# Moving the HBM copies of w_in's quarters, and setting the last three of w_out's inner sums behind g's sums

## The chip, the cores and the metric

The kernel runs on one core of a Trainium2 chip. Its engines work side by side, each through its own instructions in order: TensorE (PE in the profile) multiplies matrices, VectorE (DVE) and GpSimd (POOL) do elementwise work, ScalarE (ACT) does activations and copies, SyncE (SP) only issues transfers. Transfers (DMAs) are issued from the queues of SP, GpSimd or ScalarE. An instruction that waits for another engine or for a transfer holds up whatever stands behind it on its own engine. The metric is the device time of one execution in microseconds (us), as a median over runs.

## The reference

A retention layer over 4 batches, 8 heads, 768 steps and a head size of 64, whose output, laid out as 3072 tokens by 512, is the input of a feed-forward block with a quick GELU:

```python
for t in range(S):
    state = gamma[None, :, None, None] * state + np.einsum('bhd,bhe->bhde', k[:, :, t], v[:, :, t])
    y[:, :, t] = scale * np.einsum('bhd,bhde->bhe', q[:, :, t], state)
x = y.transpose(0, 2, 1, 3).reshape(B * S, H * D)
h = x @ w_in                                  # 3072 x 512 by 512 x 2048
g = h * (1.0 / (1.0 + np.exp(-1.702 * h)))
out = g @ w_out                               # 2048 x 512
```

Everything is computed in float32.

## The kernel before

**Blocks.** The tokens are worked through in six blocks (m = 0 to 5) of four chunks each. A chunk is 64 time steps of two batches; `step(j, f)` (L368) lets TensorE attend to chunk j and finish chunk f, with VectorE's mask, state and output operations (L316, L366, L328, L345) and GpSimd's `kd` (L272) and state ageing (L357) beside it; `turn(j)` (L238) has VectorE transpose q and k (L251). Each block needs an up product (x with w_in, giving h), a GELU on ScalarE (L391, giving g) and a down product (g with w_out).

**Fast products.** The products use a seven-product scheme (Strassen in Winograd's form). So sums of quarters of the operands have to be made: of w_in by `sums_w1` (GpSimd, L429), of x by `sums_x` (GpSimd, L439), of w_out by `sums_w2` (VectorE, L445), of g by `sums_g` (VectorE, three operations for each pair of row blocks, L454 to L458) and `sums_g_late` (GpSimd, one for each pair, L460). Blocks 0 and 1 come up in another way during the opening, and go down by `down(m)` (L672); blocks 2 to 5 come up by `up(d)` (L465), d = 0 to 3, a quarter of the product each, and go down by `down49` (L553), which uses the scheme twice over, 49 products, and needs an inner set of sums of w_out.

**`down(m)`.** It is a list of 28 units: seven products (n = 0 to 6) by four quarters d, each unit four matmuls `pd<-W,G` on TensorE (L709; each matmul leaves two records in the profile). The seven are (g0,w0), (g1,w2), (g3,w1), (g0,w5), (g3,w4), (g2,w6) and (g1,w3). After the units of the third (units 8 to 11) `sums_g` is emitted for the pair of that quarter, as it changes g3, g2 and g0 in place; the fourth product (units 12 to 15) reads that g0. After the units of the fifth (units 16 to 19) `sums_g_late` is emitted, which changes g1 for the last product (units 24 to 27). When a product is complete, ScalarE copies it (`keep`, L681) or VectorE adds it to an output tile (`put`, L685, or L716 for `t`), and GpSimd's queue sends the tile out (L686). Output tiles `o` have two buffers. The tile `t`, which the last output sum of a block reads, lies in buffer s1; so does p1, ScalarE's copy of the first product of `up(0)` (L479).

**Inner sums and their transfers.** `inner_w2(i)` (L516), i = 0 to 6, makes three VectorE sums (L522) of one of w_out's seven quarters in X[:, 4:7], and a transfer of 768 KB writes them to HBM, to W2D[i]. All seven share X[:, 4:7], so the sums of i + 1 wait for the transfer of i. The list `INNER` names the block and unit behind which each stands. `inner_w2_t3(i)` (L526) makes a fourth sum in place (L529). In blocks 2 to 5 GpSimd's queue brings W2D back in turn into a tile called ring (L545), which lies where W1B[0] lay; a tile `own`, for sums of g, lies where W1B[1] lay.

**w_in's second half.** W1B[0] and W1B[1] hold the last two of w_in's four parts with their sums. In block 1 `sums_w1` makes these, and SP copies each to HBM (L437, 1792 KB, to W1D). Blocks 3 to 5 fetch them from there (L883, L887).

**Order.** TensorE's instructions run in the order in which they are written. On the other engines a scheduler places them by when it takes them to be ready, except that those passed to `keep_in_program_order` keep theirs. Between units, block 1 also has five pieces of the retention layer (behind units 0 or 2, 5, 11, 16 and 21), and `sums_x` behind the last.

Of the kernel before, what the change touches and what calls it, by code (L numbers as in the profile page):

```python
# [28 lines left out]
def kernel(  # L29
# [29 lines left out]
    pe, act, dve, pool, sp = nc.tensor, nc.scalar, nc.vector, nc.gpsimd, nc.sync  # L59
# [13 lines left out]
    NP = NFF // 2  # L73
# [17 lines left out]
    W1B = [late.tile([P, 2, 7, 2, P], F32, name=f"W1B{i}", tag=f"late{i}") for i in range(2)]  # L91
    W1D = [dram.tile([P, 2, 7, 2, P], F32, name=f"W1D{i}") for i in range(2)]
# [19 lines left out]
    def w1(p):  # L112

        return (W1A, p) if p < NP // 2 else (W1B[p // 2 - 2], p % 2)
# [278 lines left out]
    def g(m, p, s):  # L393

        if m:
            return G[:, p:p + 2, s, :]
        if s < 3:
            t, q1 = w1(p)
            return t[:, q1:q1 + 2, 4 + s].rearrange("p a c f -> p a (c f)")
        return X[:, 4 + p // 2] if p < 6 else G0  # L400
# [28 lines left out]
    def sums_w1(p):  # L429
        t, q1 = w1(p)  # L430
        w = [t[:, q1:q1 + 2, s] for s in range(7)]
        pool.tensor_add(w[4], w[2], w[3])
        pool.tensor_sub(w[6], w[0], w[2])
        pool.tensor_sub(w[5], w[4], w[0])
        pool.tensor_sub(w[2], w[1], w[5])
        if p >= NP // 2:
            sp.dma_start(W1D[p // 2 - 2], W1B[p // 2 - 2])  # L437

    def sums_x():  # L439
        pool.tensor_sub(X[:, 4], X[:, 2], X[:, 0])  # L440
# [19 lines left out]
    def sums_g_late(m, p):  # L460
        a = [g(m, p, s) for s in range(2)]
        tc.keep_in_program_order(pool.tensor_sub(a[1], a[1], a[0]))
# [49 lines left out]
    def w2q(w):  # L512

        return [W2[:, w, u::2, e * P:(e + 1) * P] for u in range(2) for e in range(2)]

    def inner_w2(i):  # L516

        b11, b12, b21, b22 = w2q(ORDER[i][1])
        t = []
        for k, a in enumerate((b12, b22, b21)):  # L520
            t.append(X[:, 4 + k].rearrange("p c (d e) -> p (c d) e", e=P))
            tc.keep_in_program_order(dve.tensor_sub(t[k], a, t[k - 1] if k else b11))  # L522
        tc.keep_in_program_order(sp.dma_start(
            W2D[i].rearrange("p k d e -> p (k d e)"), X[:, 4:7].rearrange("p k c t -> p (k c t)")))

    def inner_w2_t3(i):  # L526
# [21 lines left out]
    def begin_ring():  # L548

        ring = late.tile([P, 7, 4, P], F32, name="ring", tag="late0")  # L550
        return ring, {i: stream(ring, i) for i in range(2)}
# [120 lines left out]
    def down(m):  # L672

        acc, kept = {}, {}
        b, t0 = m * CB // NC * 2, m * CB % NC * D
        rows = out.rearrange("(b t) (e c) -> e t b c", b=B, c=EH)[:, t0:t0 + TH, b:b + 2, :] \
            .rearrange("e (h p) b c -> h e p b c", p=P)

        def keep(name, tag, src):
            kept[name] = one.tile([P, 2, EH], F32, name=name, tag=tag)  # L680
            act.activation(kept[name], src, AF.Copy)  # L681

        def put(th, e, a, b):
            o = two.tile([P, 2, EH], F32, name="o")
            dve.tensor_add(o, a, b)  # L685
            tc.keep_in_program_order((pool if m < NB - 1 else act).dma_start(rows[th, e], o))  # L686

        def last_part(d, halves={}):

            n = d // (NP // 4)  # L690
            if d % (NP // 4) == 0:
                halves[n] = ps.tile([P, EH], F32, name="pd", tag="xy"[n])
            for p in range(NP // 2 * (d % 2), NP // 2 * (d % 2 + 1)):
                pe.matmul(halves[n], g1(m, p, 1)[:, n * P:(n + 1) * P], W2[:, 3, p, :], start=(p == 0), stop=(p == NP - 1))
            if d % 2:
                o = two.tile([P, 2, EH], F32, name="o")
                dve.tensor_add(o[:, 0], halves[n], kept["t"][:, n])
                act.dma_start(rows[0, 1][:, n], o[:, 0])

        def part(key, sa, sb, new, last, d, then):  # L700
            if m == NB - 1 and key == "x2":
                last_part(d)
                return
            if d == 0 and new:
                acc[key] = ps.tile([P, 2, EH], F32, name="pd", tag=key[0])
            p0 = acc[key]
            for p in range(2 * d, 2 * d + 2):
                for n in range(2):
                    pe.matmul(p0[:, n, :], g1(m, p, sa)[:, n * P:(n + 1) * P], W2[:, sb, p, :],  # L709
                              start=(new and p == 0 and n == 0), stop=(last and p == NP - 1), skip_group_check=True)  # L710
            if d == NP // 2 - 1:
                then(p0)

        def then_p5(y):
            kept["t"] = one.tile([P, 2, EH], F32, name="t", tag="s1")
            dve.tensor_add(kept["t"], y, kept["u"])  # L716

        def then_p7(x):
            keep("vv", "s3", x)
            put(1, 0, acc["y1"], kept["vv"])  # L720
            put(1, 1, acc["y2"], kept["vv"])

        P_ = [("x", 0, 0, True, False, lambda x: keep("p1", "s1", x)),
              ("y0", 1, 2, True, True, lambda y: put(0, 0, y, kept["p1"])),
              ("y1", 3, 1, True, True, lambda y: None),
              ("x", 0, 5, False, False, lambda x: keep("u", "s2", x)),
              ("y2", 3, 4, True, True, then_p5),
              ("x", 2, 6, False, True, then_p7),
              ("x2", 1, 3, True, True, lambda y: put(0, 1, y, kept["t"]))]
        todo = []  # L730
        for n, (key, sa, sb, new, last, then) in enumerate(P_):
            for d in range(NP // 2):
                def unit(key=key, sa=sa, sb=sb, new=new, last=last, d=d, then=then, n=n):
                    part(key, sa, sb, new, last, d, then)
                    if n == 2:
                        sums_g(m, 2 * d)
                    if n == 4:
                        sums_g_late(m, 2 * d)
                todo.append(unit)
        return todo  # L740

# [81 lines left out]
    for name, i in [("0a", 0), ("0b", 1)] + [(str(p), 2 * p) for p in range(1, NFF)]:  # L823
        n = Narrow(i)
# [37 lines left out]
    """.split():  # L862
        works[name]()
    ordered[0] = False
    INNER = [(0, 19), (0, 22), (0, 25), (1, 0), (1, 4), (1, 10), (1, 15)]
    for m in range(NB):
        between = []
        if m == 0:
            between = [lambda: turn(2 * CB), lambda: step(2 * CB), lambda: None, lambda: None, lambda: turn(2 * CB + 1)]
        elif m == 1:  # L870
            between = [lambda: (decay(2 * CB), load(2 * CB + 1, "v"))]
            for j in range(2 * CB + 1, 3 * CB + 1):
                between.append(lambda j=j: (step(j, j - 1), j < 3 * CB and turn(j + 1)))
        elif 1 < m < NB - 1:
            last = min((m + 2) * CB, NCH - 1)
            for j in range((m + 1) * CB + 1, last + 1):
                between.append(lambda j=j: (step(j, j - 1), j < last and turn(j + 1)))
            if last == NCH - 1:
                between.append(lambda: step(None, NCH - 1))
        if m > 1:  # L880
            if m > 2:
                W1B[:] = [late.tile([P, 2, 7, 2, P], F32, name=f"W1B{i}", tag=f"late{i}") for i in range(2)]
                pool.dma_start(W1B[0], W1D[0])  # L883
            for d in range(NP // 2):
                up(d)
                if d == 0 and m > 2:
                    pool.dma_start(W1B[1], W1D[1])  # L887
                if d == 0 and m < NB - 1:
                    turn((m + 1) * CB + 1)
                if d == NP // 2 - 2:  # L890
                    ring = begin_ring()
                if m == 2:
                    for i in range(2 * d, min(7, 2 * d + 2)):
                        inner_w2_t3(i)
        for n, unit in enumerate(down(m) if m < 2 else down49(m, *ring)):
            unit()
            if m == 0 and n < NP and n % 2:
                sums_w2(n - 1)
            if m == 0 and NP <= n < 3 * NP // 2:
                sums_w2_t3(2 * (n - NP))  # L900
            if m == 1 and n % 8 == 3:
                sums_w1(n // 4)
            if (m, n) in INNER:
                inner_w2(INNER.index((m, n)))
            if between and (n in (2, 5, 11, 16, 21) if m == 1 else n % 3 == (1 if m else 2)):
                between.pop(0)()
                if m == 1 and not between:
                    sums_x()
            if 1 < m < NB - 1 and n == 11:
                sums_x()  # L910
# [46 lines left out]
```

## Time and profile before

| What | us |
|---|---|
| Median of 10 runs (lowest, highest) | 678.0 (676.32, 681.2) |
| The profiled execution, its time | 679.76 |
| The profiled execution, first to last instruction (span) | 677.6 |
| TensorE busy | 656.7 |
| VectorE busy | 434.3 |
| GpSimd busy | 171.0 |
| ScalarE busy | 157.1 |
| Block 1's `down` on TensorE | 211.4 to 280.3 |
| `up(0)` of block 2 starts | 280.3 |
| `down49` of block 2 starts | 328.7 |

The page and the answers to questions about the trace give times in us from the start of the span. A row of a timeline is: start, duration, engine, line, operation, output tile, input tiles, shapes, number of records and, in brackets, how long the engine had been idle and who ended that. A row of a table by stretches gives, for each stretch, its length, the busy time (and number of records) of PE, weight loads, VectorE, ScalarE and GpSimd, then the granted clock of TensorE (1.00 is full), the share of the DMA engines and GB/s. A row of a table of waits gives who waited for whom, the total, how often and the longest.

### The profile page before, as it was taken

The page shows a single profiled execution, that of the slowest core. Times are in us where ns is not written, and L with a number is a line of the kernel's source. Part 1 is how long each engine was busy: PE and PEld are TensorE (multiplying, and loading weights), DVE is VectorE, ACT ScalarE, POOL GpSimd, SP SyncE. Part 2 cuts the span into 40 slices and gives each one's busy share as a digit, 9 for nine tenths or more (in the row PEclk, how much of TensorE's full clock was granted, in tenths as well). Part 3 has the DMA queues.
Part 4 walks back from the last instruction along what each step waited for, and adds up shares of the span by engine and source line. Part 5 has one row for each costly group of instructions (what it writes and reads, how often), then busy time and mean ns, then how long its engine had stood idle before and what let it go on. Part 6 is the DMA issues. An engine that isn't in the chain of part 4 may idle for free.

```text
span 677.6 us, 15326 instructions
## 1 busy us (share of the span) xinstructions
PE 656.7 (97%) x6502; PEld 569.5 (84%) x6502; DVE 434.3 (64%) x614; ACT 157.1 (23%) x313; POOL 171.0 (25%) x189
## 2 busy tenths in 40 slices
PE   6899999999999969999999999999999999999997
PEld 3788864747888848888999988999988999988997
DVE  4688880879836495345788255798254896254865
ACT  5665523321000000133200133200133200133210
POOL 3000000020278232500155700255700244500000
PEclk9799999999999979999999999999999999999999
DMA  9989732332303865412167573177572153502142
GB/s 182 217 197 247 189 120 85 132 90 46 67 27 151 313 166 116 101 28 77 56 172 186 135 230 101 48 176 180 116 243 99 51 155 111 216 33 94 47 156 94
DMA packets 143781, 88.97 MB, mean 131 GB/s; under 512 B 129473, under 2 KB 130753, under 8 KB 142689
## 3 DMA queue, kind: packets, MB, share of 16 engines
q1 hardware_dynamic: 134656, 48.33, 30.8%
q0 software_dynamic: 6752, 38.42, 16.0%
q10 hardware_dynamic: 2304, 1.25, 0.6%
q8 instruction: 51, 0.84, 0.5%
q14 instruction: 18, 0.14, 0.1%
HBM read 72.37 MB, written 15.47 MB: 130 GB/s over the span
## 4 chain that ended last, share of the span: by engine, by line
PE 93%; DVE 4%; DMA 2%; issue 0%; SPq 0%; ACTq 0%
PE pq L576 26%; PE px L472 16%; PE pd L709 13%; PE py L472 12%; PE ph L412 8%; PE ph L425 8%; PE pt L248 2%; PE pa L287 2%; DMA kn_in<-in_k_dram 2%; PE py L310 2%; PE pa L295 2%; PE py L304 2%; DVE G L457 1%; DVE G L458 1%; DVE X L522 0%; DVE G L456 0%
## 5 line engine op out<-in xcount | busy, mean ns | idle before, releaser
L576 PE MATMUL pq<-W,G 128*128 128x128 f32 x672 | 80.2, 276 | 0.0
L576 PEld LDWEIGHTS pq<-W,G 128*128 128x128 f32 x672 | 77.6, 192 | 0.6
L545 POOL DMA_DIRECT2D ring<-W2D x28 | 15.5, 554 | 233.2 <-PE px L472 122.9
L709 PE MATMUL pd<-W,G 128*128 128x256 f32 x224 | 54.9, 406 | 6.7 <-DVE G L458 6.6
L472 PE MATMUL px<-X,W1A 128*128 128x256 f32 x256 | 59.8, 379 | 0.0
L472 PE MATMUL px<-X,W1B 128*128 128x256 f32 x256 | 59.8, 379 | 0.0
L576 PE MATMUL pq<-ring,own 128*128 128x128 f32 x448 | 59.8, 276 | 0.0
L709 PEld LDWEIGHTS pd<-W,G 128*128 128x128 f32 x224 | 45.1, 204 | 15.1 <-DVE G L458 4.5
L576 PEld LDWEIGHTS pq<-ring,own 128*128 128x128 f32 x448 | 54.5, 192 | 0.4
L472 PEld LDWEIGHTS px<-X,W1B 128*128 128x128 f32 x256 | 48.6, 190 | 6.6
L472 PEld LDWEIGHTS px<-X,W1A 128*128 128x128 f32 x256 | 48.4, 190 | 6.5
L472 PE MATMUL py<-X,W1A 128*128 128x256 f32 x192 | 45.4, 379 | 0.0
L472 PE MATMUL py<-X,W1B 128*128 128x256 f32 x192 | 45.4, 379 | 0.0
L391 ACT ACTIVATE G<-G 128x512 f32<-128x512 f32 x48 | 30.2, 630 | 52.0 <-DVE G L482 33.4
L472 PEld LDWEIGHTS py<-X,W1A 128*128 128x128 f32 x192 | 36.5, 190 | 5.0
L472 PEld LDWEIGHTS py<-X,W1B 128*128 128x128 f32 x192 | 36.5, 190 | 5.0
L490 DVE TENSOR_TENSOR t<-py,u 128x512 f32<-128x512 f32 x16 | 11.1, 692 | 35.4 <-PE py L472 35.4
L479 ACT ACTIVATE p<-px 128x512 f32<-128x512 f32 x16 | 9.6, 598 | 94.3 <-PE px L472 94.3
L412 PE MATMUL ph<-X,W1A 128*128 128x256 f32 x128 | 29.3, 383 | 1.3 <-DVE X L345 0.7
L576 PE MATMUL pq<-ring,G 128*128 128x128 f32 x224 | 29.6, 275 | 0.0
L576 PE MATMUL pq<-W,own 128*128 128x128 f32 x224 | 29.6, 275 | 0.0
L504 DVE TENSOR_TENSOR G<-G 128x512 f32<-128x512 f32 (+2 forms) x24 | 12.3, 514 | 25.7 <-ACT G L391 25.7
(202 smaller groups left out, 1174.1 us busy)
## 6 DMA issues: line engine op xcount, KB each, us to landing
ring<-W2D POOLq DMA_DIRECT2D x28, 768.0 KB, 4.9
W1B<-W1D POOLq DMA_DIRECT2D x6, 1792.0 KB, 9.3
W<-in_moe_w_in_dram SPq DMA_DIRECT2D x12, 512.0 KB, 6.3
W2D<-X SPq DMA_DIRECT2D x7, 768.0 KB, 3.6
W<-in_moe_w_out_dram SPq DMA_DIRECT2D x10, 512.0 KB, 4.7
out_dram<-o POOLq DMA_DIRECT2D x20, 256.0 KB, 4.1
v_in<-in_v_dram SPq DMA_DIRECT2D x64, 64.0 KB, 3.1
q_sq<-in_q_dram SPq DMA_DIRECT2D x128, 32.0 KB, 2.2
```

What stands on the lines that cost most here:

```text
L248: pe.matmul(p[n][HALF[r], s, :], x[n][:, HP * r + s, :], ident, start=True, stop=True)
L287: pe.matmul(pa[HALF[w], u, 0, s, :], kt[HALF[u], w, s, :], qt[HALF[u], w, s, :], start=True, stop=True)
L295: pe.matmul(pa[HALF[u], w, 1, s, :], kd[HALF[w], HP * u + s, :], vn[HALF[w], HP * u + s, :], start=True, stop=True)
L304: pe.matmul(py[HALF[o], u, 1, 2 * w + s2, :], old[HALF[u], w, 2 * s2 + o, :], qt[HALF[u], w, 2 * s2 + o, :], start=True, stop=True)
L310: pe.matmul(py[HALF[o], w, 0, 2 * u + s2 if f < 2 * CB else 2 * s2 + u, :], vn[HALF[w], HP * u + s, :], a[HALF[w], u, s, :], start=True, s ...
L391: pin(act.activation(g, h[:, i], AF.Gelu_apprx_sigmoid))
L412: pe.matmul(h[:, ab], w, X[:, 2 * th + c // 2, c % 2, :], start=(ab == 0 and c == 0), stop=(c == 3), skip_group_check=True)
L425: pe.matmul(h, w, X1[:, c // 2:4:2, c % 2, :], start=(c == 0), stop=(c == 3))
L472: pe.matmul(acc[:, u, :], t[:, q1 + u, sa, c, :], X[:, sb, c, :], start=(start and u == 0 and c == 0), stop=(stop and c == 1), skip_group_ ...
L545: pool.dma_start(c, W2D[i])
L576: pe.matmul(p0[:, j, :], a[:, d], w[:, d], start=(new and j == 0 and d == 0), stop=(d == NP // 2 - 1), skip_group_check=True)
L709: pe.matmul(p0[:, n, :], g1(m, p, sa)[:, n * P:(n + 1) * P], W2[:, sb, p, :], start=(new and p == 0 and n == 0), stop=(last and p == NP - ...
```

## The change

Three things move; nothing is added to or taken from the arithmetic.

1. The two copies of W1B to W1D leave `sums_w1` in block 1. SP now issues them in block 2, behind `up(0)` and `up(1)` in the program.
2. `sums_g_late` is emitted for all four pairs behind unit 19, in blocks 0 and 1, where each pair stood behind its own unit, 16 to 19.
3. The list `INNER` changes: inner sums 2 to 6 stand behind other units, the last three behind units 12, 15 and 18 of block 1 (before: 4, 10 and 15). The transfers of the last three are issued from GpSimd's queue, in program order, instead of SP's.

```diff
@@ def sums_w1(p):
         pool.tensor_sub(w[2], w[1], w[5])
-        if p >= NP // 2:
-            sp.dma_start(W1D[p // 2 - 2], W1B[p // 2 - 2])
@@ def inner_w2(i):
-        tc.keep_in_program_order(sp.dma_start(
+        tc.keep_in_program_order((sp if i < 4 else pool).dma_start(
             W2D[i].rearrange("p k d e -> p (k d e)"), X[:, 4:7].rearrange("p k c t -> p (k c t)")))
@@ def down(m):
                     if n == 2:
                         sums_g(m, 2 * d)
-                    if n == 4:
-                        sums_g_late(m, 2 * d)
+                    if n == 4 and d == 3:
+                        for p in range(0, NP, 2):
+                            sums_g_late(m, p)
@@ the blocks
-    INNER = [(0, 19), (0, 22), (0, 25), (1, 0), (1, 4), (1, 10), (1, 15)]
+    INNER = [(0, 19), (0, 22), (0, 26), (1, 2), (1, 12), (1, 15), (1, 18)]
...
                 if d == NP // 2 - 2:
                     ring = begin_ring()
+                if m == 2 and d < 2:
+                    tc.keep_in_program_order(sp.dma_start(W1D[d], W1B[d]))
                 if m == 2:
```

Line numbers up to 435 are the same in both; behind it the new file's are two lower up to `sums_g_late`'s call in `down`, one lower from there to the blocks' up products, and one higher behind those.

## Prediction

> **What bounds the kernel now.** I read the page's busy shares and its 40 slices first, then what TensorE waits for around the one slice in which its clock falls, and then each engine's timeline there.
>
> ```profile
> PE 656.7 (97%) x6502; PEld 569.5 (84%) x6502; DVE 434.3 (64%) x614; ACT 157.1 (23%) x313; POOL 171.0 (25%) x189
> ...
> PEclk9799999999999979999999999999999999999999
> ```
>
> TensorE fills 97% of the span. After the opening there is one weak slice, the fifteenth (237 to 254 us), inside block 1's `down`. TensorE's waits from 155 to 300 us are these two alone:
>
> ```profile
> PE pd L709 <- DVE G L458: 6.6, 2, 3.5
> PE pd L709 <- DVE W1B L458: 0.3, 1, 0.3
> ```
>
> TensorE's timeline (start, duration, records, idle before) shows what the hole costs:
>
> ```profile
> 235.90 0.65 PE L310 MATMUL py<-at,v_in 64*64 64x64 f32 x32
> 240.07 7.68 PE L709 MATMUL pd<-W,G 128*128 128x256 f32 x24 [3.52 <-DVE G L458]
> 250.80 6.71 PE L709 MATMUL pd<-W,G 128*128 128x256 f32 x16 [3.06 <-DVE G L458]
> 257.44 0.69 PE L287 MATMUL pa<-qT,kT 64*64 64x64 f32 x32
> ...
> 280.32 1.89 PE L472 MATMUL px<-X,W1A 128*128 128x256 f32 x8
> ```
>
> From 236.55 (235.90 + 0.65) to 257.44 are 20.89 us for 40 records, units 12 to 16. Elsewhere 48 records take 10.4 us, 1.73 a unit of eight, so five units are worth 8.65. The hole is 20.89 - 8.65 = 12.24 us: the named waits of 6.6, short ones inside the first row, and a slow clock, which the table by stretches shows (the number after POOL's is the granted clock):
>
> ```profile
> 240.00:242.00 2.00, 1.93 (x5) 1.60 (x6) 1.97 (x2) 0.00 (x0) 1.92 (x2) 0.50 0.94 243
> 252.00:254.00 2.00, 2.00 (x7) 1.53 (x6) 2.00 (x4) 0.00 (x0) 1.91 (x2) 0.50 0.40 82
> ```
>
> Each idle stretch of 3 us or more is followed by half clock: finer stretches put it at 240 to 243 and 250 to 256.6. Why g's sums are late stands in VectorE's timeline:
>
> ```profile
> 226.94 0.69 DVE L522 TENSOR_TENSOR X<-W 128x512 f32<-128x512 f32 x1 [6.52 <-DMA W2D<-X]
> ...
> 234.65 0.69 DVE L522 TENSOR_TENSOR X<-W 128x512 f32<-128x512 f32 x1 [1.85 <-DMA W2D<-X]
> ...
> 237.79 0.68 DVE L456 TENSOR_TENSOR G<-G 128x512 f32<-128x512 f32 x1
> ```
>
> VectorE works in order. Inner sums 3 wait for W2D2's transfer (issued 218.97, landed 7.9 later, next to a W1D copy), inner sums 4 for W2D3's, and g's sums stand behind both. From 234.65 to 255.4 VectorE hardly rests: it is late by its order, not for want of room.
>
> **The change, part by part.** The times are in the profiled execution's frame. By the compiled order nothing moves on any engine before g's sums of block 1 except W1D's two issues.
>
> *W1D out of block 1.* W2D2 then leaves SP's queue without a 1792 KB neighbour. W2D1, issued at 210.83 without one, released VectorE at 214.71: 3.9 us. So inner sums 3 start at 222.7 instead of 226.94 and end about 225.2 (2.1 to 2.5, a GpSimd operation beside them). Six operations of the step, one `inner_w2_t3` and y0's output follow at 0.6 to 0.7 each: 230.3. Inner sums 4 are gone from there, so g's four triples start at 230.3 instead of 237.79; at 2.05 a triple (237.79 to 239.84), and 0.7 for kd beside one, they end near 232.4, 234.4, 237.1 and 239.2. TensorE wants them from 236.55 on at 1.73 steps, the last at 241.7. Least margin: 2.5 us. The whole hole closes, and everything on TensorE moves 12.24 us earlier if nothing else holds it: block 1's unit 24 to 261.1, `up(0)` from 280.32 to 268.1.
>
> *W1D in block 2.* The two issues stand on SP behind q's and k's loads for the next step, which in the profile end at 304.66; with the sum below (4.7 earlier), W1D goes at 300. Queued behind them are kn and v loads that wait for GpSimd's kd anyway. The ring reuses W1B[0] and is issued near 312.3 (317.05 before); its first reader stands 14 us after that (331.34), `own`, which takes W1B[1]'s place, 12 (328.87). A copy took 11.8 at most. Cost 0; the cover is the third and fourth quarter of the up product.
>
> *Inner sums 4 to 6, on GpSimd's queue.* After g's sums six operations of the step (3.9) bring VectorE to 243.0; inner sums 4 end at T4 = 245.1. From there it is a chain: transfer, sums 5 (2.1), transfer, sums 6 (2.7 with one t3 between), issue. The trace has no W2D write from GpSimd. Its bounds: 3.9 us from end of sums to next sums (SP's W2D1), and 5.5 (GpSimd's reads of the same 768 KB for the ring land in 4.9 to 5.2, plus hand-over). GpSimd's 256 KB writes land in 2.6 to 2.9, ACT's in 2.1, so its queue adds about 0.6: I take 3.9 + 0.7 = 4.6. Then sums 5 end at 251.8, the step's six operations at 255.7, sums 6 run from 256.4 to 259.1. The transposes that TensorE's step wants at 256.0 are done at 254.5.
>
> The skill has a price of its own: the Trainium skill, "DMA: Bandwidth & Descriptors", "Anatomy of one DMA — SWDGE (gpsimd) path", puts such a transfer at 2.0 us plus bytes over 436 GB/s, here an estimate of 3.8, and the total below would be near 672.
>
> Against this change speaks another page. GpSimd's output issues at 208.18 and 210.18, with VectorE busy, landed in 2.6 as with VectorE idle. The Trainium skill, "SBUF — State Buffer", "SBUF: two separate sides", warns that a transfer issued from GpSimd starves while VectorE holds the port they share, 620 ns becoming 3100. By it the two transfers waited for would grow by some 2.5 each and the total would be an estimate of 680; the row decides.
>
> *g's late sums behind them.* GpSimd also works in order. Its new queue is: issue W2D4, W2D5, W2D6, then the four late sums, kd, the four `sums_x`, then y1's and y2's outputs. Before, the late sums were over at 257.8 and this row set the rest:
>
> ```profile
> 253.09 4.67 POOL L462 TENSOR_TENSOR G<-G 128x512 f32<-128x512 f32 x3
> 271.49 1.27 POOL L440 TENSOR_TENSOR X<-X 128x512 f32<-128x512 f32 x1 [13.73 <-DVE X L345]
> ...
> 276.95 1.48 POOL L686 DMA_DIRECT2D out_dram<-o  x2
> ```
>
> Now W2D6's issue (0.55) follows 259.1, and the late sums take 1.57 each (4.67 / 3): the first ends at 261.45, the fourth at 266.1. Unit 24 wants the first at 261.1: **0.35 us** lost, and the others just keep ahead of 1.73 steps. Then kd (1.05) to 267.2, `sums_x` (5.3, between 5.05 at 1.26 each and the 5.5 of this row) to 272.5. X5 is wanted later than it comes. But y1's output is issued at 272.5, and lands 2.65 later, 275.15. That is what is late next: block 1's last output sum writes the buffer this transfer reads.
>
> ```profile
> 280.52 0.69 DVE L685 TENSOR_TENSOR o<-pd,t 128x512 f32<-128x512 f32 x1 [0.17 <-PE pd L709]
> ...
> 282.30 0.60 ACT L479 ACTIVATE p<-px 128x512 f32<-128x512 f32 x1 [8.02 <-PE px L472]
> ```
>
> Before, the transfer (276.95 + 2.6) landed 0.9 ahead of that sum. The sum reads `t` in buffer s1, and `up(0)`'s first copy p1 writes s1, so ScalarE waits for it; TensorE's third product adds onto px and waits for p1. New chain: landing 275.15, sum to 275.9, p1 to 276.6, TensorE at 276.65. It was ready at 268.4 + 3.45 = 271.85: **4.8 us** lost. At such an idle time the clock falls; the two falls of the hole halved it for 2.8 and 6.3 us, a loss of 1.4 to 3.2: I take **2.4**.
>
> *Sum.* -12.24 + 0.35 + 4.8 + 2.4 = -4.7. The span goes from 677.6 to 672.9; this execution took 679.76, 2.16 more than its span and 1.8 above the median of 678.0 shown. Taken off the median: **673.3 us**.
>
> With the transfer at 3.9 the first late sum ends at 260.1, nothing is lost at unit 24 and 3.9 later: 672.0. With 5.5, unit 24 loses 2.2: 675.1. The clock's bounds add 1 each way: 671 to 676 for the likeliest case.
>
> **The rivals.**
> (A) *The hole closes and nothing takes its place*: 678.0 - 12.2 = 665.8. For it: GpSimd is busy 25% and X5 was ready 8 us before its product (275.67 against 283.77). Against it: the 0.9 us to spare of y1's transfer, when GpSimd's chain gains only some 4.5 of TensorE's 12.2.
> (B) *The W2D chain itself becomes the bound, slower.* One mechanism: VectorE's sums 5 and 6 wait for GpSimd's transfers, with the step's operations behind them. W2D2 landed in 7.9 once; at 8.1 from sums to sums, TensorE's step waits 1.75 at 256, unit 24 then 5.65 with a slow clock (2.4), and the 4.8 and 2.4 stay: 17.0 lost against 12.24, 682.8. It decides from about 6.1, where gain and loss cancel. Against it: that 7.9 lay next to a W1D copy, which has left.
> (C) *W1D comes too late for the ring*: every us beyond 21 from issue to landing costs one; at 25 it is 677.3. Against it: 11.8 is the most seen.
> That the order stays as it was can be excluded by the compiled order.
>
> **How the numbers follow.** A measurement of this kernel tells about 0.3% from no change: 676.0 to 680.0 is the same. Forecast 0.68 (0.60 below 676.0, 0.08 above), A 0.12, B 0.16 (0.05 same, 0.11 slower), C 0.04 (half and half). Faster 0.72, same 0.15, slower 0.13. The range runs from 667, between A and the forecast, to 679, into B; outside lie most of A and the worse half of B.
>
> **What would show it.** Right: no wait of pd on VectorE's L456; g's first sum of block 1 near 230; a wait of VectorE's last output sum (L683) for an out_dram transfer of about 6 us, one of px for ScalarE's p of 4 to 5, then half clock near 277; a wait of pd for GpSimd's L460 under 2.5; `up(0)` starting at 268 to 269. Wrong: px without a wait (A), L520 waiting 6 us or more for W2D twice (B), pq waiting for the ring (C), or g's sums still after 236.5.

## The result, and the profile after

| | before | after |
|---|---|---|
| Median, us (lowest, highest; runs) | 678.24 (675.92, 681.94; 49) | 673.34 (670.66, 676.97; 14) |
| Ratio after to before, 95% interval | | 0.9926 (0.991, 0.9941) |
| Profiled execution: time, span | 679.76, 677.6 | 676.21, 674.5 |
| TensorE: block 1's first step to `up(0)` | 58.45 | 46.32 |
| TensorE: `up(0)` to `down49` of block 2 | 48.35 | 55.30 |
| TensorE: `down49` of block 2 to the next `up` | 52.18 | 53.25 |
| TensorE: from there to the end of the span | 296.75 | 297.62 |

The change makes the kernel 4.9 us faster; 673.3 was forecast. The page's engine totals and clock come first:

```profile
PE 655.7 (97%) x6502; PEld 569.2 (84%) x6502; DVE 439.9 (65%) x614; ACT 157.0 (23%) x313; POOL 171.8 (25%) x192
...
PEclk9799999999999999799999999999999999999999
```

The weak slice has moved from the fifteenth to the seventeenth, from block 1's `down` to the start of block 2's `up`. VectorE has the same 614 instructions and is busy 5.6 us longer: one of them takes long. TensorE's waits from 155 to 330 us:

```profile
PE px L470 <- ACT p L477: 3.0, 1, 3.0
PE py L470 <- DVE o L683: 0.4, 1, 0.4
PE pd L707 <- DVE W1B L456: 0.3, 1, 0.3
```

The 6.6 us of waits for g's sums are gone, and px waits for ScalarE's p1, as forecast. TensorE's timeline at that place (the end of block 1, then `up(0)`):

```profile
257.87 10.63 PE L707 MATMUL pd<-W,G 128*128 128x256 f32 x48
268.33 1.89 PE L470 MATMUL px<-X,W1A 128*128 128x256 f32 x8
270.57 1.99 PE L470 MATMUL py<-X,W1A 128*128 128x256 f32 x8 [0.35 <-DVE o L683]
275.54 3.75 PE L470 MATMUL px<-X,W1A 128*128 128x256 f32 x8 [2.97 <-ACT p L477]
279.09 3.18 PE L470 MATMUL py<-X,W1A 128*128 128x256 f32 x8
```

`up(0)` starts at 268.33 (280.32 before). Its third product was due 3.45 behind that, at 271.78, and comes at 275.54: 3.76 late. The two products from there take 6.56 to 282.10, where two at full clock take 3.45: another 3.11. The table by stretches has the clock (the number ahead of the last two):

```profile
276.00:278.00 2.00, 2.00 (x6) 1.55 (x6) 0.18 (x1) 0.63 (x1) 0.00 (x0) 0.50 0.68 196
```

VectorE's timeline shows what was not forecast:

```profile
261.32 0.69 DVE L345 TENSOR_TENSOR X<-py,tmp 128x512 f32<-128x512 f32 x1
261.93 7.99 DVE L527 TENSOR_TENSOR W<-W 128x512 f32<-128x512 f32 x1
269.84 1.27 DVE L683 TENSOR_TENSOR o<-pd,vv 128x512 f32<-128x512 f32 x2
271.04 0.68 DVE L527 TENSOR_TENSOR W<-W 128x512 f32<-128x512 f32 x1
273.99 0.69 DVE L683 TENSOR_TENSOR o<-pd,t 128x512 f32<-128x512 f32 x1 [2.28 <-DMA out_dram<-o]
```

A sum of `inner_w2_t3` takes 7.99, where the two of the same line at 257.60 and 258.80 took 0.68 and 0.69. It depends on nothing late: the row has no wait. y1's and y2's output sums (L683, two records) stand behind it, and are what the transfer of y1 sends out. In the same time GpSimd does this:

```profile
259.18 0.53 POOL L521 DMA_DIRECT2D W2D<-X  x1 [6.49 <-DVE X L520]
259.73 4.96 POOL L460 TENSOR_TENSOR G<-G 128x512 f32<-128x512 f32 x4
264.66 1.03 POOL L272 TENSOR_TENSOR kd<-kn_in,cold 128x512 f32<-128x512 f32 x1
265.66 1.26 POOL L438 TENSOR_TENSOR X<-X 128x512 f32<-128x512 f32 x1
...
268.11 1.26 POOL L440 TENSOR_TENSOR X<-X 128x512 f32<-128x512 f32 x1
269.45 1.60 POOL L441 TENSOR_TENSOR X<-X 128x512 f32<-128x512 f32 x1
270.99 1.51 POOL L684 DMA_DIRECT2D out_dram<-o  x2
```

From 259.73 to 269.37 (268.11 + 1.26) GpSimd works without a pause; at 269.45 there is one of 0.08, and VectorE's sum ends 0.55 after the last of the row. So y1's output had two holders: VectorE, which made the tile at about 270.5, and GpSimd's order, which sent it at 270.99. Which of them sets the time was the open question.

### The profile page after: what moved, and what is told of

Read it like the earlier page. It is cut to its first block, busy times and chain, and to the rows that moved or that the text cites. A ratio compares the mean times of both kernels' runs of the same rounds, so it can differ in the third digit from the quotient of the medians.

```text
span 674.5 us, 15330 instructions
## 1 busy us (share of the span) xinstructions
PE 655.7 (97%) x6502; PEld 569.2 (84%) x6502; DVE 439.9 (65%) x614; ACT 157.0 (23%) x313; POOL 171.8 (25%) x192
## 4 chain that ended last, share of the span: by engine, by line
PE 89%; DMA 4%; DVE 3%; SPq 2%; POOL 1%; issue 1%; ACT 0%; ACTq 0%; DVEq 0%; POOLq 0%
PE pq L574 26%; PE px L470 16%; PE py L470 12%; PE pd L707 10%; PE ph L425 8%; PE ph L412 8%; PE pt L248 2%; SPq L137 2%; PE pa L287 2%; PE pa L295 2%; PE py L310 2%; PE py L304 1%; DMA W2D<-X 1%; DMA v_in<-in_v_dram 1%; DMA kn_in<-in_k_dram 1%
## 5 line engine op out<-in xcount | busy, mean ns | idle before, releaser
L470 PE MATMUL px<-X,W1A 128*128 128x256 f32 x256 | 61.9, 388 | 3.0 <-ACT p L477 3.0
L707 PE MATMUL pd<-W,G 128*128 128x256 f32 x224 | 49.6, 381 | 0.0
L707 PEld LDWEIGHTS pd<-W,G 128*128 128x128 f32 x224 | 42.2, 190 | 5.9
L470 PE MATMUL py<-X,W1A 128*128 128x256 f32 x192 | 46.8, 388 | 0.4 <-DVE o L683 0.4
```

The source lines that it names most:

```text
L470: pe.matmul(acc[:, u, :], t[:, q1 + u, sa, c, :], X[:, sb, c, :], start=(start and u == 0 and c == 0), stop=(stop and c == 1), skip_group_ ...
```

## The experiments

Line numbers in profiles are those of the changed kernel; in e8, which has the two lines of `sums_w1` again, they are two higher. In the expectations, theory T is the prediction's own: GpSimd's order alone delays y1's output. Theory L adds VectorE's held sum. Each kernel is compared with runs of the kernel before on the same chip (medians there 678.2 to 679.2). No kernel leaves out any of the computation.

| Run | Median, us | Ratio to before, 95% interval | `up(0)` to `down49`, us | px waits, us |
|---|---|---|---|---|
| after | 673.34 | 0.9926 (0.991, 0.9941) | 55.30 | 3.0 |
| e1_t_in_u | 673.24 | 0.9926 (0.9898, 0.9954) | 53.65 | 2.4 |
| e2_out_act | 672.7 | 0.9906 (0.9875, 0.9937) | 52.75 | 1.9 |
| e3_out_act_t3 | 669.75 | 0.9869 (0.9841, 0.9898) | 48.35 | none |
| e4_w1d_alone | 676.37 | 0.9961 (0.9943, 0.9979) | 48.34 | none |
| e5_late_back | 672.54 | 0.9908 (0.9888, 0.9929) | 52.85 | 2.5 |
| e6_late_out | 670.4 | 0.988 (0.986, 0.9901) | 48.36 | none |
| e7_t3_pin | 672.72 | 0.9915 (0.9888, 0.9942) | 52.69 | 2.4 |
| e8_w1d_back | 678.4 | 0.9995 (0.9978, 1.0012) | 53.93 | 3.0 |
| e9_gap | 671.06 | 0.9889 (0.986, 0.9918) | 50.83 | 1.9 |
| e10_best_again | 668.77 | 0.9852 (0.982, 0.9883) | 48.34 | none |
| e11_sums_x_order | 671.43 | 0.9903 (0.9867, 0.9939) | 51.37 | 1.9 |

**Does the buffer of `t` carry the wait?** e1 puts `t` where p1 doesn't go:

```diff
-            kept["t"] = one.tile([P, 2, EH], F32, name="t", tag="s1")
+            kept["t"] = kept["u"]
```

> The changed kernel with t made in place in u's buffer (s2), so that up(0)'s first copy p1 (buffer s1) no longer waits for block 1's last output sum. Theory T (what is left is y1's output transfer, behind GpSimd's queue, holding that sum and through s1 the copy p1 and TensorE): the wait of px for ScalarE's p (3.0 us) and the half clock behind it (3.1 us in the changed kernel) go, though the output sum still waits about 2 us for the transfer; 673.3 - 6 = 667.5 us, at least 5 faster than the changed kernel. Rival R2 (the wait is GpSimd's sums of x themselves, X5 not ready): the same wait stays, 673 us. Rival R3 (the clock falls on its own there): no more than 3 us gained.

A miss. p1 is no longer held, but the wait moves one product on. ScalarE's timeline of e1:

```profile
271.45 0.60 ACT L477 ACTIVATE p<-px 128x512 f32<-128x512 f32 x1 [8.19 <-PE px L470]
278.69 0.63 ACT L391 ACTIVATE G<-G 128x512 f32<-128x512 f32 x1 [6.65 <-DVE G L480]
279.23 0.58 ACT L484 ACTIVATE u<-px 128x512 f32<-128x512 f32 x1
```

p1 comes at 271.45, but VectorE's L480 stands behind the output sum that waits for the transfer (4.23 us in its timeline), ScalarE's GELU waits for L480, and the copy u that TensorE wants next stands behind the GELU: px waits 2.4 for u. The buffer is only one of the paths from the late output sum to TensorE. What must move is the transfer.

**Who holds the transfer?** e2 lets ScalarE issue it, so that GpSimd's order is out of its way:

```diff
-            tc.keep_in_program_order((pool if m < NB - 1 else act).dma_start(rows[th, e], o))
+            tc.keep_in_program_order((act if m == 1 and th == 1 else pool if m < NB - 1 else act).dma_start(rows[th, e], o))
```

> The changed kernel with y1's and y2's outputs of block 1 issued from ScalarE's queue instead of GpSimd's. T in its simple form (GpSimd's order alone makes the transfer late): the transfer leaves as soon as its sum is done, near 263, nothing waits for it, 667.5 us. Rival L (VectorE is late too: its L527 sum took 7.99 us, from 261.93 to 269.92, while GpSimd summed without a break, and the output sum stands behind it): the transfer leaves at 270.5 instead of 271.0 and lands some 0.6 sooner, so px waits 1.5 to 2.0 instead of 3.0; between 670 and 672.5 us by whether the clock still falls.

px still waits 1.9 us, and VectorE's sum is still held:

```profile
262.50 7.96 DVE L527 TENSOR_TENSOR W<-W 128x512 f32<-128x512 f32 x1
270.39 1.28 DVE L683 TENSOR_TENSOR o<-pd,vv 128x512 f32<-128x512 f32 x2
```

ScalarE issues at 271.10, as soon as the tile is made. T alone is refuted: with GpSimd out of the way 4.4 of the 6.95 us that the stretch behind `up(0)` had lost stay (52.75 against 48.35). e3 also takes the `inner_w2_t3` sums out of that stretch. Kept in program order, they run in block 2:

```diff
-        dve.tensor_sub(b12, b22, b12)
+        tc.keep_in_program_order(dve.tensor_sub(b12, b22, b12))
```

> As the run before, and VectorE's fourth inner sums of w_out (L527) kept in program order, which sets all seven behind block 1, into the up products of block 2. L: VectorE has no operation with two SBUF operands beside GpSimd's late sums any more, makes y1's output at about 262, the transfer has landed by 265, px does not wait, 667 us, 3 to 5 faster than the run before. Simple T: no difference from the run before.

Now the output sums stand at 266.12, ScalarE issues at 268.23, px has no wait, and `up(0)` to `down49` is 48.35, as in the kernel before. The size is not wholly the expected one: this profiled execution started block 1's `down` at 215.4 where the changed kernel's did at 211.6. e10 repeats the kernel on another occasion:

> The kernel e3 again, on the same chip and beside the same runs of the kernel before as e9: 669 to 670.5 if its 669.75 was its own, and no wait of px; 671 to 673 if that median was luck of its chip. If theory L holds, e9 and this lie within 1.5 us of each other.

668.77, just under the range, and no wait of px: the gain is the kernel's own. e9, whose turn comes below, is not within 1.5 us of it (671.06). e7 is the counterpart, e3's edit of the sums without e2's of the queue.

> The changed kernel with VectorE's fourth inner sums moved behind block 1, but the outputs left on GpSimd's queue. If both holders are needed (GpSimd's order and VectorE's held sum tie at 271.0 and 270.5): VectorE makes y1's output by 263, but it leaves GpSimd near 271 all the same, px waits 2.5 to 3.3 as in the changed kernel, 673 us. If VectorE's held sum alone is the cause: no wait, 669.75 us as with both edits.

```profile
264.81 1.27 POOL L438 TENSOR_TENSOR X<-X 128x512 f32<-128x512 f32 x1
...
268.61 1.26 POOL L441 TENSOR_TENSOR X<-X 128x512 f32<-128x512 f32 x1
269.82 1.51 POOL L684 DMA_DIRECT2D out_dram<-o  x2
```

VectorE made the tiles from 262.22 on, but GpSimd's queue sent them at 269.82 all the same, and px waits 2.4. Either holder alone keeps most of the loss (52.69 here, 52.75 in e2, against 48.35); only freeing both gives it back.

**The late sums.** e5 puts each pair's late sum behind its own unit again (change 2 undone, 1 and 3 kept); e6 is e5 with e2's edit.

```diff
-                    if n == 4 and d == 3:
-                        for p in range(0, NP, 2):
-                            sums_g_late(m, p)
+                    if n == 4:
+                        sums_g_late(m, 2 * d)
```

> The changed kernel with g's late sums emitted pair by pair again, as before the change. By the compiled order two of the four go ahead of W2D4's issue, one between W2D5 and W2D6, one behind W2D6. T: GpSimd's tail behind W2D6 is then one late sum, kd and the sums of x, which now wait for W2D6 to land; y1's output leaves near 269.7 instead of 271.0 and VectorE is let go in the gap before the sums of x; px waits about 2 instead of 3.0, 670 to 672 us. Rival N (where the late sums stand is no matter, since nothing waits for them): 673 us with the same wait. Rival P (two late sums beside inner sums 4 hold VectorE and push the chain back): W2D4 leaves 1.5 or more later, px waits 3 or more.

> As the run before, and y1's and y2's outputs of block 1 from ScalarE's queue. T with L: VectorE's output sum is made by 265, ScalarE sends it at once, it has landed by 268; no wait of px, the whole hole stays closed, like the run with ScalarE's outputs and the fourth sums moved (669.75): 667 to 670 us. If VectorE is held all the same, its L527 takes over 5 us and px waits about 2: 671 to 673 us.

One late sum now runs between the last two W2D issues, one behind the last, and GpSimd's row is short. VectorE in e5:

```profile
263.49 0.69 DVE L527 TENSOR_TENSOR W<-W 128x512 f32<-128x512 f32 x1
264.11 1.28 DVE L683 TENSOR_TENSOR o<-pd,vv 128x512 f32<-128x512 f32 x2
```

The same sum takes 0.69, which frees VectorE; GpSimd's order still holds the issue to 270.37, and px waits 2.5. In e6 ScalarE issues it at 267.34, and px has no wait. The price of the other order is at the step, where TensorE waits 0.6 and 0.6 (0.6 and 0.5 in e6) for VectorE, whose inner sums came later; e3 has no such wait. e5's time, 672.54, can't be told from the changed kernel's 673.34 (the intervals of the ratios overlap), so no gain from change 2 can be measured; what it did was to put together the row beside which VectorE was held.

**What each part of the change earns.** e4 is the kernel before with the W1D copies alone moved; e8 the changed kernel with the W1D copies back in block 1.

> The kernel before with the W1D copies moved into block 2 and nothing else. By my steps: inner sums 3 start at 222.6 and inner sums 4 still stand ahead of g's sums, which start at about 235 and end near 247 with the step's operations among the last triple; TensorE waits about 1.5 in units 12 to 14 and 3.5 at unit 15, with a slow clock behind it: 4 to 7 us of the 12.2 are gained, 671 to 674 us. GpSimd's tail is early, so no wait of px for p. Rival W (W1D beside W2D2 was all there was to it): the hole closes wholly, 666 us. Rival O (the order in VectorE is all): the hole stays, 677 to 678 us.

> The changed kernel with the W1D copies back in block 1, the other two parts as changed. My steps: inner sums 3 wait for W2D2 until about 226.9, g's sums start at 234.6 instead of 230.3 and end near 243.5; TensorE waits about 2 in units 12 to 15, the chain of W2D4 to W2D6 starts 4 us later, unit 24 waits 1.5 to 3 for GpSimd's late sums, and px about 3 for p with the slow clock: 4 to 8 us lost against the changed kernel, 677 to 681 us. Rival (the order in VectorE alone is what the change brings, the copies are no matter): 673 us.

TensorE's waits in e4:

```profile
PE pd L707 <- DVE G L456: 5.7, 3, 3.1
PE pd L707 <- DVE W1B L456: 0.3, 1, 0.3
```

With W1D out of the way g's sums are still late: 5.5 of the hole's 12.1 us are won (52.95 in place of 58.45 to `up(0)`), and nothing is lost behind it. The span of its profiled execution is 4.3 shorter, its median 2.8: less than was expected, in size but not in kind. In e8 the hole shrinks by 8.7 (to 49.79), the tail takes 5.6 of it back, and later stretches 1.1. Its profiled execution keeps a gain of 2.2 in the span, but over all its runs nothing is left: 0.9995. So neither edit closes the hole alone, and the new order without the move of the copies is worth nothing that can be measured. No run tells the new list of inner sums from the move of three transfers to GpSimd's queue.

**What holds VectorE?** e9 puts one small transfer issue on GpSimd between the third and the fourth late sum of e2:

```diff
                             sums_g_late(m, p)
+                            if m == 1 and p == 4:
+                                tc.keep_in_program_order(pool.dma_start(W1D[0][:, 0, 0, 0, :], W1B[0][:, 0, 0, 0, :]))
```

> The kernel e2 (y1's and y2's outputs of block 1 issued by ScalarE) with one small transfer (64 KB of W1B[0] to W1D[0], written again later with the same data) issued by GpSimd between the third and the fourth late sum; GpSimd then makes no sum for about 0.5 us near 264. Theory L (VectorE's two-operand sum of L527 is held by GpSimd's unbroken row of sums and freed by the first pause): L527 starts near 262.5 and ends near 264.5, 2 us and not 8; the output sums of y1 follow, ScalarE issues near 267, no wait of px; 669.5 to 671. Rival M (L527 is held for a reason of its own, by data or by a transfer, or a pause for an issue doesn't free it): L527 takes 8 us or more again, px waits about 2, 672.5 to 673.5.

GpSimd's timeline and VectorE's, both of e9:

```profile
258.30 3.73 POOL L460 TENSOR_TENSOR G<-G 128x512 f32<-128x512 f32 x3
261.98 0.57 POOL L739 DMA_DIRECT2D W1D<-W1B  x1
262.57 1.28 POOL L460 TENSOR_TENSOR G<-G 128x512 f32<-128x512 f32 x1
...
267.24 1.26 POOL L440 TENSOR_TENSOR X<-X 128x512 f32<-128x512 f32 x1
268.57 1.61 POOL L441 TENSOR_TENSOR X<-X 128x512 f32<-128x512 f32 x1
```

```profile
260.50 8.56 DVE L527 TENSOR_TENSOR W<-W 128x512 f32<-128x512 f32 x1
```

The issue does not free VectorE. The sum lasts 8.56, longer by 0.6, the length of the issue, and ends at 269.06, again 0.56 behind the end of GpSimd's L440 (268.50). Rival M's duration came, but its cause did not: a wait for data or a transfer would not have moved with GpSimd's row. Its time did not come either: 671.06 lies between the two forecasts, with the clock at 1.00 behind the wait (it was 0.50 in e2). e11 exchanges two of the four sums of x, to move the pause ahead:

> The kernel e2 with the second and third of GpSimd's sums_x exchanged (X5 = X3 - X4 straight behind X4; the same four sums). In e9 VectorE stayed held through GpSimd's issue of a transfer, and in e2 and e9 alike it came free where GpSimd's fourth sum of x waits 0.07 us for the third. Theory N (VectorE's two-operand sum is held until GpSimd first waits for a result of its own; an issue doesn't count): the first such wait moves ahead by one or two sums, L527 ends 1.2 or 2.5 us sooner in GpSimd's frame, so it lasts 5.4 to 6.8 us and ends with the first pause among the sums of x; px's wait for ScalarE falls from 1.9 to under 0.8; 670 to 671.5. Rival M (something else holds it): it ends where it did, near the start of the last sum of x, 7.9 to 8.0 long, px waits 1.9, 671 to 673.

The exchange did not move it: L440 and L439 ran without a pause, and GpSimd paused again ahead of the last sum. VectorE's 7.97 ended there once more (269.60, for a row that ends at 269.05). So this run agrees with both readings and doesn't tell whether GpSimd's wait for its own result is what counts; a pause put inside the late sums was not tried. Nor did any run move the point at which VectorE's sum comes up: in all six held cases it is 0.95 to 0.97 us into the second late sum.

## Why the prediction was right, and where it was not

**The hole.** Forecast 12.24, measured 12.13 (58.45 - 46.32). The steps in it hold: g's sums began at 230.25 (forecast 230.3) and ended at 239.38 (239.2), and no wait of pd on them is left. e4 and e8 show that the move of the copies and the new order are both needed for it, as the sum had them.

**W1D in block 2: nothing.** SP issued the copies at 299.58 (forecast 300), and TensorE had no wait for the ring. The later stretches of the changed kernel are 1.07 and 0.87 us longer than before, and the only wait of TensorE there is one of 0.8 us for nothing that the profile shows. From `down49` to the next `up`, kernels that all have the W1D edit vary by as much (52.18 in e5, 52.73 in e4, 53.42 in e7), so it is put down to no edit, and stays open.

**The W2D chain.** From the end of one set of sums to the start of the next 4.67 and 4.42 us, where 4.6 was taken. The transfers from GpSimd landed in 4.0 to 4.1. The estimate of 3.8 from the Trainium skill, "DMA: Bandwidth & Descriptors", was near the 4.0 to 4.1; the delay that the other page made possible for GpSimd's transfers was not seen. By the Trainium skill, "SBUF — State Buffer", "SBUF: two separate sides", it was not due: the page measured that delay beside a VectorE tensor_copy, and counts tensor_tensor, which these sums are, among the operations that showed none.

**The late sums and unit 24.** Mis-sized: 1.57 each was taken from a row in which VectorE's sums ran between them; alone they took 1.24, so unit 24 lost nothing (forecast 0.35) and y1's output was issued at 270.99, not 272.5. The prediction's sum also lets the first late sum end at 261.45, where its own terms (259.1, 0.55 and 1.57) give 261.2.

**The tail.** Forecast 4.8 late and 2.4 of clock, 7.2 together; measured 3.76 and 3.11, and 6.95 for the stretch. The chain from the landing over the last output sum and p1 to TensorE is as forecast. What failed is the step "That is what is late next", which named one holder, GpSimd's queue. The runs showed a second one of nearly the same length. VectorE was taken to be idle and ready by then; in fact it was held until 269.9 by GpSimd's row of sums, the same late sums that the change had put together. The prediction's own sign shows it: VectorE's last output sum was to wait about 6 us for the transfer, and waited 2.28, as VectorE was at work on what it had been kept from. Had GpSimd's queue been the only cause, e2 would have got rid of the wait. The time came out right since the holder that it had not seen let go half a microsecond ahead of the one that it named, and that is luck. So is the agreement to 0.1 us: the changed kernel's runs lie between 670.66 and 676.97. A reader who had acted on the prediction's cause alone would have moved the queue (e2) and kept more than half of the loss.

**The rivals.** A (nothing takes the place of the hole) falls for the changed kernel; e3 and e10 come near it from the other side, at 0.9869 and 0.9852 against the 0.982 that 665.8 to 678.0 would be. B and C did not come: the W2D transfers from GpSimd took 4.1 at most, no ring wait was seen. The stretches of the profiled execution add up: 0.15 - 12.13 + 6.95 + 1.07 + 0.87 = -3.1, its span's change; the first is block 1's first step starting later. Without the two unexplained ones it is -5.0, close to the medians' -4.9; whether other executions lack the two isn't shown, but this one, at 676.21, took 2.9 more than the median.

**A version that beats both.** e10's kernel (the same as e3's), the change with y1's and y2's outputs on ScalarE's queue and all seven `inner_w2_t3` sums set into block 2: 668.77 against 679.14 of the kernel before beside it.

## What to carry to other kernels

A closed hole moves everything behind it earlier, and the next thing to be late is found by asking of each engine on the way what it does at the new time, not only of the one that issues the late transfer. Before two engines' elementwise work is put side by side, look whether both take their operands from the same memory: at one place here a VectorE sum stood still for the rest of a row of GpSimd's sums (7.99 in place of 0.68), while at others it lost the time of one GpSimd operation at most (a sum of g took 1.53). Such a hold shows in the profile as a long operation and not as a wait, so read the durations too. Try the suspected holders one by one and then together, since two that end at the same time each look innocent when the other one is left.

## What the runs showed of the hardware

**A two-operand VectorE sum stood still for a whole row of GpSimd's sums.** L527 (W from W and W, no operand from TensorE's outputs) took 7.96 to 8.56 us in the six kernels (after, e1, e2, e8, e9, e11) in which GpSimd worked through four late sums, kd and three sums of x without a pause, and 0.69 in e5, where GpSimd paused from 263.62 to 265.03. In the same stretch VectorE's sums with one operand from TensorE's outputs (`at`, `tmp`, X) ran in their 0.68 beside the late sums. The hold ended 0.55 us behind the end of the row each time, and the issue of a transfer (e9) did not end it. When VectorE came through, GpSimd paid: its last sum of x took 1.60 there, and 1.26 in e7, where VectorE had nothing to do then.

A row without pauses does not always do this. In the kernel before, VectorE came through after one GpSimd operation:

```profile
253.66 1.75 DVE L522 TENSOR_TENSOR X<-W 128x512 f32<-128x512 f32 x1
...
272.72 1.27 POOL L441 TENSOR_TENSOR X<-X 128x512 f32<-128x512 f32 x1
272.75 1.78 DVE L529 TENSOR_TENSOR W<-W 128x512 f32<-128x512 f32 x1 [1.34 <-PE pd L709]
273.94 1.73 POOL L442 TENSOR_TENSOR X<-X 128x512 f32<-128x512 f32 x1
```

The first came up in a row of three late sums that ran from 253.09 to 257.76, and was done at 255.41. The second, of the same kind as the one held later, ended 0.55 behind L441, though L442 followed at once. They came up 0.57 and 0.03 us into a GpSimd sum, the six held ones 0.95 to 0.97. Whether that point decides is not shown.

The Trainium skill, "SBUF — State Buffer", "SBUF: two separate sides", says that a VectorE operation with two inputs in that memory and a GpSimd operation that reads it lock each other out, for one whole instruction. The rows of the kernel before agree. In the changed kernel the hold was longer than the page has it: the sum came up during the second late sum, and stayed held over six changes from one GpSimd instruction to the next, up to the pause of 0.08 us. That the lock is what held it is the page's word; no run here shows the lock itself. The forecast had read that page for its word on transfers and had not asked it about the sums.

**A short idle time cost as much again as clock in some runs, and no clock in others.** In the changed kernel 3.3 us of named waits were followed by 6 us at half clock, 3.1 us lost. In e2 waits of 1.9 and 0.3 were followed by half clock too (0.50 from 276 to 278), and the stretch was 4.4 longer than undisturbed (52.75 against 48.34). In e9 (1.9) and e11 (1.9 and 0.6) the granted clock stayed at 1.00, and the stretch was 2.5 and 3.0 longer (50.83 and 51.37). Waits of nearly the same length cost 2.2 us beyond themselves in the one case and, with no fall of the clock, some 0.5 in the others, and a forecast needs both ends.
